# Packed attention and a gated feed-forward layer: halves of 288 tokens, a new order of steps, four stores from two engines

## The chip, the cores and the metric

The kernel runs on one core of a Trainium2 chip. The metric is the time of one execution on the device in microseconds (us); for the kernel before it is the median of three runs.

TensorE (PE) multiplies matrices and puts the results into PSUM banks; VectorE (DVE), ScalarE (ACT) and GpSimdE (POOL) work on elements; DMA transfers are issued by instructions on the queue of an engine, here mostly that of SyncE (SP).

## What is computed

```python
def sm_attn(qq, kk, vv):
    s = scale * np.matmul(qq, kk.transpose(0, 1, 3, 2))
    a = np.exp(s - np.max(s, axis=-1, keepdims=True))
    return np.matmul(a / (np.sum(a, axis=-1, keepdims=True) + 1e-09), vv)

p_packed = sm_attn(p, k, v)             # 32 pack queries per head
out = sm_attn(q, p_packed, p_packed)    # q: 8 batches, 8 heads, 576 tokens, 64 wide
x = out.transpose(0, 2, 1, 3).reshape(4608, 512)
h = x @ w_in                            # 512 x 2048
g = h * (1.0 / (1.0 + np.exp(-1.702 * h)))
return g @ w_out                        # 2048 x 512
```

Everything is float32. The weights reach the kernel as 64-bit words, which it converts.

## The kernel before

**Precision.** Each large product is made of three matmuls: an operand is split into an upper part, rounded to the matmul's type (`g_upper`, a cast, L175 on ScalarE and L177 on VectorE), and a lower part, the rest (`g_lower`, a subtraction, L848, on VectorE or GpSimdE), and upper x upper, upper x lower and lower x upper are added up in PSUM.

**Tiling.** A batch is 576 tokens. Its attention runs with all 8 heads at once: scores of the 32 pack queries (`scores1`, matmuls L369), their softmax, the packed values, then the scores of q against these (`scores2_mm`, L624, into the two banks of `hh`), transposed on VectorE (`scores2_turn`, L632) for the second softmax. `m_chunk` (L590) multiplies the packed values with `w_in`, so that h comes straight from the softmax weights. The q tokens of a batch are worked in two **halves**, `NH = (NA, NB_)` = 256 and 320 tokens.

Batch 0 runs while the weights are still loading, with steps of its own (`h_mm`, `h_tanh`, `h_gate`, `out_mm`). From batch 1 on, a **round** n = 2 to 15 is one half (batch n // 2, half n % 2), and in it a **pair** p = 0 to 7 is 256 of the 2048 columns of h. For each pair:

- `hp_mm` (twice): 6 matmuls (L705, in `h_terms`) into `hh`, of which there is one, with two banks;
- `hp_tanh` (ScalarE, L811) reads `hh` and writes the buffer of g in SBUF; `hp_gate` (VectorE, L698) multiplies it with `hh`, and after that `hh` is free;
- `hp_over` (a DMA on SP, L821) copies 64 tokens of the 320 to DRAM (`over_kept`), 56 times in all, in the odd rounds;
- `sums_1` to `sums_3` (L833, L837, L841), `g_upper`, `g_lower` prepare the operands; `product` (L870) multiplies 256 tokens by blocks with `w_out` into the four banks `acc`, in seven block products (15 pairs in four plain ones, `plain`);
- at the end of a round `take_1` to `take_6` (L894 to L918) add up `acc` in SBUF and `keep` (L924) stores 256 tokens.

The 64 left-over tokens of four batches are 256 again: rounds `('over', 0)` and `('over', 1)` read them back (`over_in`, L825) and end in `keep_over` (L929), four stores of 64 tokens each.

The buffers of g are a ring of two: pair i uses buffer i % 2, so `hp_tanh` of pair p + 2 waits until pair p's `hp_over` has been read out.

**What sets the order.** No scheduler: all steps stand in a table `order` of (step, arguments), written out in full, and are issued in that order. An engine takes its instructions in the order of the table, as does SP its DMAs: loads of q, k and v (`load`, L215 to L229) and of the weights (`load_w`, L259), their conversion (`begin_w`, ScalarE, L267; `join_w`, VectorE, L280), `w_kept` (a copy of `w_in` in DRAM, read back for every batch by `win_in`, L301), the transposed scores by way of DRAM (`aside`, L494 and L505) and all stores. `warm` (L181) is a matmul of the identity whose result nobody reads.

Of the kernel before, what the change touches and what calls it, by code (L numbers as in the profile page):

```python
# [19 lines left out]
P = 128  # L20
# [4 lines left out]
def kernel(  # L25
    ctx: ExitStack,
    tc: tile.TileContext,
    q0: bass.AP,
    q1: bass.AP,
# [10 lines left out]
    B = q0.shape[0]  # L40
# [5 lines left out]
    NH = (NA, NB_)  # L46
    S = NA + NB_
    REST = NB_ - NA
    NF = DF // P
# [29 lines left out]
    A = [region(4 * NA), region(4 * NB_)]  # L79
# [3 lines left out]
    X = [region(n) for n in (S, 2 * NB_, 2 * NB_, 2 * NB_, 2 * NB_)]  # L83
# [7 lines left out]
    DEC = region(3 * FC + 3 * NB_ + 64)  # L91
# [3 lines left out]
    SPARE = region(DM)  # L95

    G_RAW = 2 * NB_ + 4 * P
    G_PART = 7 * P + REST
# [64 lines left out]

    def rows(eo):
        return slice(eo * D, (eo + 1) * D)
# [24 lines left out]
    def kq_view(what, b):  # L190
# [7 lines left out]
        if what == "k":  # L198
            kq["p", b] = words(at, NP * NPK).rearrange("p (j n) -> p j n", n=NPK)
            at += NP * NPK  # L200
            n = (KF, S - KF)
        else:
            n = NH
# [5 lines left out]
    def load(what, b, part):  # L209
# [402 lines left out]
    def x2(b, half, eo=None):  # L612
        t = x_tile(X2.get((b, half), (0, 1)[half]), 2 * NH[half])
        return even_odd(t, eo)

    def xt(b, half, eo=None):
        t = x_tile(XT.get((b, half), (2, 4)[half]), 2 * NH[half])
        return even_odd(t, eo)

    def scores2_mm(b, half, banks):  # L620
        banks = [bank(i) for i in banks]
        for j in range(NP):
            for eo in range(2):
                nc.tensor.matmul(  # L624
                    banks[eo][32 * j : 32 * j + 32, : NH[half]], pt(b)[rows(eo), j, :],
# [4 lines left out]
    def scores2_turn(b, half, eo):  # L630
        t = st["bank", 2, b, half][eo]
        nc.vector.transpose(x2(b, half, eo), t[:, : NH[half]])  # L632
# [11 lines left out]
    def small2(name, b, half, eo):  # L644
        return even_odd(small((name, half), 2 * NH[half] // NPK), eo)
# [27 lines left out]
    def a_part(b, half, part, eo=None):  # L673
        at = A_FIRST if (b, half) == (0, 0) else A[half]
        n = 2 * NH[half]
# [5 lines left out]
    def a_lower_mm(b, half, eo, i):  # L681
        st["al", b, half, eo] = t = bank(i)
        n = NH[half]
# [3 lines left out]
    def a_lower_copy(b, half, eo, engine=nc.scalar):  # L687
        move(engine, a_part(b, half, 1, eo), st["al", b, half, eo][:, : NH[half]])
# [11 lines left out]
    def h_terms(t, b, f, half):  # L700
# [9 lines left out]
    def th0(f, half):  # L710
        return words(TH0 + TH_HOME[f][half] * NB_, NH[half])
# [8 lines left out]
    def h_tanh(b, f, half):  # L720
        nc.scalar.activation(th0(f, half), st["h", f, half][:, : NH[half]], AF.Tanh, scale=1.702)

    def h_gate(b, f, half):
        g = th0(f, half)
        gate(g, g, st["h", f, half][:, : NH[half]])

    def h_part(f, half):
        return th0(f, half)[:, NH[half] - NA :]
# [43 lines left out]
    def g_lead(n):  # L772
        return REST if isinstance(n, int) and n % 2 else 0
# [31 lines left out]
    def hp_view(n, p):  # L805
        k = NH[n % 2]
# [119 lines left out]
    def keep_over(n, i, k, engine=nc.sync):  # L926
# [7 lines left out]
        (warm, 1, 1, 5), (load, 'k', 0, 0), (warm, 7, 7, 4), (load, 'k', 0, 1), (load_w, 1, 0),  # L934
        (load_w, 0, 0), (load, 'v', 0, 0), (warm, 6, 2, 5), (load, 'v', 0, 1), (warm, 5, 2, 5),
        (load, 'q', 0, 0), (warm, 3, 3, 4), (load_w, 2, 0), (warm, 0, 3, 5), (load, 'q', 0, 1),
        (scores1, 0, 0, (6, 0)), (max1_first, 0, 0), (max1_first, 1, 0), (scores1, 0, 1, (7, 1)),
        (load_w, 3, 0), (bias1_first, 1), (bias1_first, 0), (exp1_first, 0, 0), (warm, 4, 2, 4),
        (load_w, 3, 1), (max1_first, 1, 1), (exp1_first, 1, 0), (warm, 8, 3, 4), (bias1, 0, 1),
        (load_w, 4), (max1_first, 0, 1), (exp1_first, 1, 1), (turn1_first, 0, 6), (bias1, 0, 0),  # L940
        (exp1_first, 0, 1), (begin_w, 1, 0), (turn1_first, 1, 7), (turn1_first_copy, 0, dve),
        (factor_first, 1), (begin_w, 0, 0), (sum1, 0, 1), (factor_first, 0), (turn1_last_mm, 0, 6),
        (turn1_first_copy, 1), (load, 'k', 1, 0), (pack_first, 0), (sum1, 0, 0),
# [976 lines left out]
```

## Time and profile before

| | us |
|---|---|
| median of three runs | 704.24 (704.01 to 705.41) |
| the profiled execution | 705.11 |
| its span in the trace | 703.3 |
| TensorE busy | 675.4 |
| VectorE busy | 567.5 |
| GpSimdE busy | 292.3 |
| ScalarE busy | 283.2 |

The trace is of one execution, and the span runs from the first recorded instruction to the last; 1.8 us lie around it. "Busy" is the time in which an engine has an instruction under way. The granted clock (PEclk) is given as a share of full speed; its mean over the span is 0.986. A wait is put down to the engine, tile and line that released it. A duration "x12" stands for twelve instructions in a row.

### The profile page before, as it was taken

Reading aid. Unit: us, or ns where it says so; the run is one execution under the profiler, and the core shown is the slowest. Engines: PE = TensorE matmul, PEld = TensorE weight load, DVE = VectorE, ACT = ScalarE, POOL = GpSimd, SP = SyncE. Lnnn points to the kernel's source line nnn. Section 1 sums busy time; section 2 is a strip of 40 time slices with the busy share of each in tenths; the row PEclk is TensorE's granted clock in tenths of the full one; section 3 lists DMA queues with packets and bytes.
Section 4 is the critical chain, followed back from the end, with each engine's and each line's share of the span. In section 5 each row is a group of like instructions: output and inputs, shape, how many; then the busy total and the mean of one; then the engine's idle time right before and its main releaser. Section 6 shows DMA issues by size and latency. Waiting matters only on the chain.

```text
span 703.3 us, 15452 instructions
## 1 busy us (share of the span) xinstructions
PE 675.4 (96%) x6037; PEld 602.3 (86%) x6037; DVE 567.5 (81%) x1123; ACT 283.2 (40%) x561; POOL 292.3 (42%) x325
## 2 busy tenths in 40 slices
PE   8799999999999999999999999999989999999996
PEld 6477767797879888899799998899879997899996
DVE  3999798885988898876998777977689778877785
ACT  3586644432453335324433334432335224333231
POOL 1434242322785446402534335553346325444232
PEclk9699999999999999999999999999999999999999
DMA  9869666324545425524451642534543632300142
GB/s 347 356 247 315 214 188 233 92 44 138 203 129 132 137 74 204 172 69 145 146 180 65 178 133 86 206 74 164 173 143 101 192 113 80 116 31 13 46 124 61
DMA packets 79017, 103.10 MB, mean 147 GB/s; under 512 B 53920, under 2 KB 58976, under 8 KB 74336
## 3 DMA queue, kind: packets, MB, share of 16 engines
q1 hardware_dynamic: 78944, 102.12, 45.0%
q8 instruction: 47, 0.77, 0.4%
q14 instruction: 26, 0.21, 0.1%
HBM read 80.14 MB, written 21.95 MB: 145 GB/s over the span
## 4 chain that ended last, share of the span: by engine, by line
PE 46%; DVE 10%; DMA 4%; issue 2%; ACT 2%; POOL 2%; DVEq 0%; SPq 0%; ACTq 0%; POOLq 0%
PE acc L870 28%; PE hh L705 15%; DMA over<-at_float 3%; DVE at_float L698 2%; DVE at_float32r L848 2%; PE b L590 2%; ACT at_float L811 1%; DVE at_float32r L177 1%; DMA at_float<-over 1%; PE hh L624 1%; DVE at_float L900 1%; PE hh L369 1%; DVE at_float32r L605 1%; ACT at_float32r L175 1%; POOL at_float L833 1%
## 5 line engine op out<-in xcount | busy, mean ns | idle before, releaser
L870 PE MATMUL acc<-at_float32r 128*128 128x256 f32 (+1 forms) x2553 | 361.2, 293 | 2.2 <-DVE at_float L918 1.1
L870 PEld LDWEIGHTS acc<-at_float32r 128*128 128x128 f32 x2553 | 330.8, 191 | 31.0 <-issue 14.6
L705 PE MATMUL hh<-at_float32r 128*128 128x256 f32 (+1 forms) x1344 | 208.4, 299 | 5.8 <-DVE at_float L632 2.7
L705 PEld LDWEIGHTS hh<-at_float32r 128*128 128x128 f32 x1344 | 186.9, 190 | 14.4 <-DVE at_float L698 5.4
L811 ACT ACTIVATE at_float<-hh 128x512 f32<-128x512 f32 (+1 forms) x112 | 72.9, 651 | 208.1 <-PE hh L705 132.2
L175 ACT CAST at_float32r<-at_float 128x512 fp32r<-128x512 f32 (+5 forms) x199 | 110.1, 567 | 99.9 <-PE acc L870 47.0
L848 POOL TENSOR_TENSOR at_float32r<-at_float,at_float32r 128x512 fp32r<-128x512 f32 (+3 forms) x82 | 102.3, 1251 | 91.3 <-DVE at_float32r L177 45.8
L698 DVE SCALAR_TENSOR_TENSOR at_float<-at_float,hh 128x512 f32<-128x512 f32 (+1 forms) x112 | 84.0, 750 | 56.9 <-ACT at_float L811 54.6
L848 DVE TENSOR_TENSOR at_float32r<-at_float,at_float32r 128x512 fp32r<-128x512 f32 (+3 forms) x159 | 109.4, 699 | 10.5 <-ACT at_float32r L175 7.1
L177 DVE CAST at_float32r<-at_float 128x512 fp32r<-128x512 f32 (+5 forms) x126 | 56.0, 449 | 8.6 <-PE acc L870 2.9
L837 POOL TENSOR_TENSOR at_float<-at_float 128x128 f32<-128x128 f32 x52 | 27.9, 537 | 82.5 <-DVE at_float L833 72.3
L833 POOL TENSOR_TENSOR at_float<-at_float 128x256 f32<-128x256 f32 x41 | 34.1, 831 | 62.6 <-DVE at_float L698 43.0
L755 PE MATMUL acc<-at_float32r 128*128 128x512 f32 x192 | 50.5, 399 | 0.7 <-DVE at_float32r L750 0.7
L841 POOL TENSOR_TENSOR at_float<-at_float 128x128 f32<-128x128 f32 x52 | 27.5, 529 | 46.4 <-DVE at_float L837 44.3
L755 PEld LDWEIGHTS acc<-at_float32r 128*128 128x128 f32 x192 | 34.0, 188 | 12.2 <-issue 3.4
L605 DVE TENSOR_TENSOR at_float32r<-b,at_float32r 128x512 fp32r<-128x512 f32 (+1 forms) x64 | 41.9, 669 | 1.4 <-ACT at_float32r L175 1.3
L833 DVE TENSOR_TENSOR at_float<-at_float 128x256 f32<-128x256 f32 x72 | 33.7, 468 | 4.6 <-DMA at_float<-over 1.5
L175 ACT CAST at_float32r<-b 128x512 fp32r<-128x512 f32 (+1 forms) x49 | 26.8, 574 | 24.9 <-PE b L590 24.8
L705 PEld LDWEIGHTS h<-at_float32r 128*128 128x128 f32 x192 | 30.0, 203 | 7.5 <-DVE at_float L698 2.3
L705 PE MATMUL h<-at_float32r 128*128 128x256 f32 (+1 forms) x192 | 32.8, 315 | 2.5 <-DVE at_float32r L605 1.1
L590 PE MATMUL b<-at_float,at_float 64*32 64x512 f32 (+1 forms) x512 | 34.6, 586 | 0.0
L280 DVE SCALAR_TENSOR_TENSOR at_float<-at_float,at_float 128x512 uint32<-128x512 uint32 (+1 forms) x36 | 29.7, 848 | 2.1 <-ACT at_float L267 2.0
(122 smaller groups left out, 556.8 us busy)
## 6 DMA issues: line engine op xcount, KB each, us to landing
at_float<-w_kept SPq DMA_DIRECT2D x24, 1024.0 KB, 5.1
at_float<-v SPq DMA_DIRECT2D x8, 1024.0 KB, 5.8
o<-at_float SPq DMA_DIRECT2D x32, 256.0 KB, 2.7
at_float<-w_out SPq DMA_DIRECT2D x16, 511.8 KB, 5.2
at_float<-w_in SPq DMA_DIRECT2D x12, 511.8 KB, 7.5
at_float<-k_last SPq DMA_DIRECT2D x8, 640.0 KB, 6.9
at_float<-q SPq DMA_DIRECT2D x8, 640.0 KB, 5.5
at_float<-pk SPq DMA_DIRECT2D x8, 576.0 KB, 4.3
```

Of the source, the lines that this page charges most:

```text
L175: nc.scalar.copy(dst, src)
L177: engine.tensor_copy(dst, src)
L280: nc.vector.scalar_tensor_tensor(dec(n)[:, at].bitcast(U32), raw(n)[:, at, 0], 13, tops[(n + (part or 0)) % 4][:, at], op0=ALU.logical_shi ...
L590: nc.tensor.matmul(banks[eo][32 * j : 32 * j + 32, columns(part)], pt(b)[rows(eo), j, :], w[rows(eo), j, columns(part)], start=True, stop= ...
L605: nc.vector.tensor_tensor(lo, t[:, at], hi.bitcast(F32), op=ALU.subtract)
L698: nc.vector.scalar_tensor_tensor(dst, th, 1.0, h, op0=ALU.add, op1=ALU.mult)
L705: nc.tensor.matmul(t[:, : NH[half]], m_part(fc, eo, mp)[:, fo : fo + P], a_part(b, half, ap, eo), start=(n == 0), stop=(n == len(terms) - 1),)
L755: nc.tensor.matmul(acc[i], g0(f, gp)[:, i * P : (i + 1) * P], wo(f, wp), start=(start and n == 0), stop=(stop and n == 2),)
L811: nc.scalar.activation(g, h, AF.Tanh, scale=1.702)
L833: engine.tensor_tensor(dst, src, by, op=ALU.subtract)
L848: engine.tensor_tensor(lo, src, g_range(n, p, 0, which)[0].bitcast(F32), op=ALU.subtract)
L870: nc.tensor.matmul(acc[i][:, at : at + m], lhs, rhs, start=(start and k == 0), stop=(stop and k == len(pairs) - 1),)
```

## The change

Four things are changed.

1. *Halves.* Batch 0 keeps 256 and 320 tokens; from batch 1 on both halves are 288. Each half now has 32 left-over tokens in place of 0 and 64, so `hp_over` runs for every pair of all rounds: 112 copies, each of 256 pieces of 128 bytes (before 56, with pieces of 256 bytes). q comes as one array, with the left-over tokens at the front of each half.
2. *Regions.* Some regions of SBUF get other sizes to suit.
3. *The order.* The first 230 steps come from a table of another version, not from the one shown here, and the others are in a new order; the two tables part from the first step on. TensorE issues 5171 instructions in both, VectorE 1125 and then 1141, ScalarE 545 and 571, GpSimdE 330 and 290, SP 332 and 386. `g_lower` runs 159 times on VectorE and 82 times on GpSimdE before, 175 and 66 times after.
4. *Last stores.* Of the four `keep_over` of the last round, two are issued by ScalarE.

```diff
+    HALF_REST = S // 2 - NA
...
-    A = [region(4 * NA), region(4 * NB_)]
+    A = [region(2 * S), region(4 * NB_)]
...
-    SPARE = region(DM)
-
-    G_RAW = 2 * NB_ + 4 * P
-    G_PART = 7 * P + REST
+    SPARE = region(S)
+
+    G_RAW = S + 4 * P
+    G_PART = 7 * P + HALF_REST
...
+    def halves(b):
+
+        return (S // 2, S // 2) if b else (NA, NB_)
...
-        elif part == 0:
-            nc.sync.dma_start(words(at, NP * NA), q0[b])
         else:
-            nc.sync.dma_start(words(at + NP * NA, NP * NB_), q1[b])
+            m = NP * halves(b)[0]
+            a, e = (m, NP * S) if part else (0, m)
+            nc.sync.dma_start(words(at + a, e - a), q[b][:, a:e])
...
-                t[:, : NH[half]], m_part(fc, eo, mp)[:, fo : fo + P], a_part(b, half, ap, eo),
+                t[:, : halves(b)[half]], m_part(fc, eo, mp)[:, fo : fo + P], a_part(b, half, ap, eo),
...
     def g_lead(n):
-        return REST if isinstance(n, int) and n % 2 else 0
+        return HALF_REST if isinstance(n, int) else 0
...
-        k = NH[n % 2]
+        k = halves(n // 2)[n % 2]
...
     def hp_over(n, p):
         b = n // 2
-        g = hp_view(n, p)[0][:, :, :REST]
+        g = hp_view(n, p)[0][:, :, :HALF_REST]
+        r = slice(n % 2 * HALF_REST, (n % 2 + 1) * HALF_REST)
         dst = over_kept[b // 4][p].rearrange("p (j t) b r -> p j t b r", t=2)
-        nc.sync.dma_start(dst[:, :, b % 4 // 2, b % 2, :], g)
+        nc.sync.dma_start(dst[:, :, b % 4 // 2, b % 2, r], g)
...
-        (keep_over, ('over', 1), 1, 1), (keep_over, ('over', 1), 0, 1),
+        (keep_over, ('over', 1), 1, 1, act), (keep_over, ('over', 1), 0, 1, act),
```

Behind the change the same steps have line numbers that are higher by 3 to 5 (`warm` L184, `scores1` L372, `h_terms` L709, `hp_over` L826, `keep_over` L934). In the rows of the order below, `h`, `b` and `acc` are PSUM banks, and `at_float` with a number is a region of SBUF.

**TensorE at the start.** Before, 18 warm-up matmuls stand ahead of the first scores (the matmuls that read the region of k):

```order
L181 MATMUL h_73<-at_float_74 128x128
L181 MATMUL h_72<-at_float_74 128x128 x7
L181 MATMUL h_73<-at_float_74 128x128 x4
L181 MATMUL h_72<-at_float_74 128x128 x3
L181 MATMUL h_73<-at_float_74 128x128 x3
L369 MATMUL b_67<-at_float_98 32x256
L369 MATMUL acc_63<-at_float_98 32x256
```

After:

```order
L184 MATMUL h_72<-at_float_74 128x128 x7
L372 MATMUL b_67<-at_float_104 32x256
L372 MATMUL acc_63<-at_float_104 32x256
L372 MATMUL b_67<-at_float_104 32x256
L372 MATMUL acc_63<-at_float_104 32x256
```

Eleven warm-ups have gone from there.

**TensorE ahead of the first product with the weights** (L593, `m_chunk`), after; the row ahead of the warm-ups is the last of the scores of q. Before, only three warm-ups stood at this place:

```order
L627 MATMUL acc_66<-at_float_113,at_float_232 32x320
L184 MATMUL h_73<-at_float_74 128x128 x2
L184 MATMUL h_72<-at_float_74 128x128 x3
L184 MATMUL h_73<-at_float_74 128x128 x3
L184 MATMUL h_72<-at_float_74 128x128 x3
L593 MATMUL acc_63<-at_float_243,at_float_232 32x256
L593 MATMUL acc_64<-at_float_243,at_float_232 32x256
```

The warm-ups stand now between the scores of q and the product with the weights.

**SP at the start**, the loads in the order in which they are issued, before (pk is the pack queries with the first 256 keys):

```order
L221 DMA at_float_98<-pk 128x1152
L223 DMA at_float_98<-k_last 128x1280
L259 DMA at_float_108<-w_in 128x1023
L259 DMA at_float_110<-w_in 128x1023
L215 DMA at_float_112<-v 128x2048
L217 DMA at_float_113<-v_last 128x512
L227 DMA at_float_120<-q 128x1024
L259 DMA at_float_125<-w_in 128x1023
L229 DMA at_float_120<-q 128x1280
```

After:

```order
L224 DMA at_float_104<-pk 128x1152
L226 DMA at_float_104<-k_last 128x1280
L218 DMA at_float_107<-v 128x2048
L262 DMA at_float_110<-w_in 128x1023
L220 DMA at_float_108<-v_last 128x512
L232 DMA at_float_113<-q 128x1024
L232 DMA at_float_113<-q 128x1280
L262 DMA at_float_116<-w_in 128x1023
L262 DMA at_float_126<-w_in 128x1023
```

Values and q have moved ahead of two pieces of `w_in`.

**SP in round 11**, before: the copies to `over` of its pairs 0 to 3 between the loads of the next q and two stores of output:

```order
L821 DMA over_95<-at_float_350 256x1x64
L229 DMA at_float_98<-q 128x1280
L821 DMA over_95<-at_float_350 256x1x64
L924 DMA o<-at_float_1226 128x512 x2
L227 DMA at_float_98<-q 128x1024
L821 DMA over_95<-at_float_350 256x1x64 x2
```

After (the first row is its pairs 0 and 1, the `aside` rows are the reads of the transposed scores):

```order
L826 DMA over_95<-at_float_350 256x1x32 x2
L508 DMA at_float_92<-aside_5077 32x4x256
L508 DMA at_float_92<-aside_5077 32x256
L508 DMA at_float_92<-aside_5077 32x4x256 x3
L508 DMA at_float_92<-aside_5077 32x256
L826 DMA over_95<-at_float_350 256x1x32
L232 DMA at_float_104<-q 128x1152 x2
L826 DMA over_95<-at_float_350 256x1x32 x2
```

Three copies stand now ahead of the loads of q, and the stores of output have left this place.

## Rows read from the trace of the kernel before

**Rows 1.** The page: busy time, share and instructions of each engine.

```profile
PE 675.4 (96%) x6037; PEld 602.3 (86%) x6037; DVE 567.5 (81%) x1123; ACT 283.2 (40%) x561; POOL 292.3 (42%) x325
```

**Rows 2.** Windows: us, busy PE, PEld, DVE, ACT, POOL, PEclk, DMA share, GB/s.

```profile
0.00:28.40 28.40, 20.84 (x246) 15.06 (x246) 16.70 (x48) 13.38 (x38) 7.80 (x18) 0.87 0.95 373
28.40:697.70 669.30, 654.55 (x5791) 587.21 (x5791) 550.15 (x1075) 269.79 (x523) 284.45 (x307) 0.99 0.43 137
```

**Rows 3.** What TensorE waited for: us in total, times, longest us.

```profile
PE hh L624 <- DVE at_float L698: 5.0, 6, 1.5
PE hh L705 <- DVE at_float L632: 2.7, 3, 1.9
```

**Rows 4.** `hp_over`, L821: ns min/median/max of an issue; who waited (us, times).

```profile
L821 SPq DMA_DIRECT2D over<-at_float x56: 512/525/972, 151.6 to 669.6; - x56
...
  ACT at_float L811: 14.7, 4
```

**Rows 5.** Timeline of TensorE: start us, us, line, tile, [idle before, releaser].

```profile
170.79 0.45 PE L624 MATMUL hh<-at_float,at_float 64*32 64x256 f32 x8 [0.85 <-DVE at_float L698]
...
517.94 0.85 PE L705 MATMUL hh<-at_float32r 128*128 128x320 f32 x4 [1.93 <-DVE at_float L632]
```

**Rows 6.** Timeline of TensorE from 398 to 410 us.

```profile
400.60 1.60 PE L705 MATMUL hh<-at_float32r 128*128 128x256 f32 x12
402.04 1.96 PE L870 MATMUL acc<-at_float32r 128*128 128x256 f32 x15
...
405.07 1.04 PE L705 MATMUL hh<-at_float32r 128*128 128x320 f32 x6
405.96 2.31 PE L870 MATMUL acc<-at_float32r 128*128 128x256 f32 x18
```

**Rows 7.** The page: DMA issues, KB each, median us from issue to landing.

```profile
over<-at_float SPq DMA_DIRECT2D x64, 64.0 KB, 2.7
aside<-at_float SPq DMA_DIRECT2D x56, 72.0 KB, 2.5
```

**Rows 8.** Timeline of TensorE from 0 to 40 us.

```profile
1.37 7.05 PE L181 MATMUL h<-at_float 128*128 128x128 f32 x36 [1.37 <-POOL at_float masks.py:199]
8.35 0.40 PE L369 MATMUL b<-at_float 64*32 64x256 f32 x1
...
16.46 0.75 PE L624 MATMUL acc<-at_float,at_float 64*32 64x320 f32 x16
...
21.16 0.64 PE L590 MATMUL acc<-at_float,at_float 64*32 64x256 f32 x2 [2.31 <-DVE at_float L280]
```

**Rows 9.** Timeline of SP: the first two issues.

```profile
0.75 0.40 SPq L221 DMA_DIRECT2D at_float<-pk  x1
1.20 0.42 SPq L223 DMA_DIRECT2D at_float<-k_last  x1
```

**Rows 10.** DMA issues from 0 to 6 us: KB each, us from issue to landing.

```profile
at_float<-k_last SPq DMA_DIRECT2D x1, 640.0 KB, 5.0
at_float<-q SPq DMA_DIRECT2D x1, 640.0 KB, 10.1
at_float<-pk SPq DMA_DIRECT2D x1, 576.0 KB, 3.9
```

**Rows 11.** Windows, columns as in rows 2.

```profile
32.00:34.00 2.00, 2.00 (x10) 2.00 (x9) 1.75 (x3) 1.29 (x3) 1.48 (x2) 0.50 0.34 137
520.00:522.00 2.00, 2.00 (x11) 2.00 (x11) 0.61 (x1) 1.18 (x2) 0.00 (x0) 0.50 1.00 412
```

**Rows 12.** Groups by line and shape: count, busy us, mean ns, idle before.

```profile
L848 DVE TENSOR_TENSOR at_float32r<-at_float,at_float32r 128x512 fp32r<-128x512 f32 x76 | 55.6, 732 | 6.2 <-ACT at_float32r L175 3.6 <-DVE at_float32r L177 0.5
L848 POOL TENSOR_TENSOR at_float32r<-at_float,at_float32r 128x512 fp32r<-128x512 f32 x46 | 61.0, 1325 | 49.7 <-ACT at_float32r L175 24.3 <-DVE at_float32r L177 21.6 <-DMA at_float<-over 2.5
```

**Rows 13.** Timeline of SP at the end: the four stores of `keep_over`.

```profile
698.13 2.43 SPq L929 DMA_DIRECT2D o<-at_float  x4
```

**Rows 14.** Windows of 20 us, columns as in rows 2.

```profile
40.00:60.00 20.00, 20.00 (x120) 16.31 (x119) 19.53 (x42) 17.39 (x39) 8.20 (x8) 1.00 0.95 336
```

More of the change, by code (lines that the diff above doesn't have):

```diff
@@ L202, in kq_view @@
         else:
-            n = NH
+            n = halves(b)
         kq[what, b] = [
@@ L644, in small2 @@
     def small2(name, b, half, eo):
-        return even_odd(small((name, half), 2 * NH[half] // NPK), eo)
+        t = small((name, half), 20 if half else 18)
+        return even_odd(t[:, : 2 * halves(b)[half] // NPK], eo)
     def max2(b, half, eo=None):
@@ L687, in a_lower_copy @@
     def a_lower_copy(b, half, eo, engine=nc.scalar):
-        move(engine, a_part(b, half, 1, eo), st["al", b, half, eo][:, : NH[half]])
+        move(engine, a_part(b, half, 1, eo), st["al", b, half, eo][:, : halves(b)[half]])
     def a_lower(b, half, engine=nc.gpsimd):
@@ new lines @@
+        (conv_upper, 0, -1, dve),
+        (both, (scores2_mm, 3, 0, (4, 5)), (m_chunk, 3, 0, (6, 7), None)), (conv_lower, 0, 1, dve),
+        (hp_over, 5, 3), (g_lower, 5, 2, 1, dve), (keep, 4, 0), (sums_1, 5, 4, dve),
+        (g_upper, 5, 3, 0, dve), (m_upper, 3, 0, 0, None, act), (win_in, 3, 1), (product, 5, 1, 6),
+        (scores2_turn, 3, 0, 0), (g_lower, 5, 3, 0, pool), (product, 5, 2, 6),
+        (scores2_turn, 3, 0, 1), (hp_mm, 5, 5, 0), (m_upper, 3, 0, 1, None, dve),
+        (conv_lower, 0, -1, pool), (hp_mm, 5, 5, 1), (sums_2, 5, 3, dve), (max2, 3, 0),
@@ new lines @@
+        (sums_3, 9, 1, dve), (take_5, 8), (pack, 5, (6, 7)), (g_upper, 9, 1, 1, act),
+        (g_upper, 9, 0, 1, act), (keep, 8, 1), (hp_tanh, 9, 3), (g_lower, 9, 0, 1, dve),
+        (load, 'q', 5, 0), (product, 9, 0, 2), (product, 9, 1, 1), (pack_end, 5), (hp_gate, 9, 3),
+        (sums_1, 9, 2, pool), (product, 9, 0, 4), (product, 9, 0, 6), (hp_over, 9, 3),
+        (sums_2, 9, 2, dve), (hp_mm, 9, 4, 0), (g_lower, 9, 1, 1, dve), (product, 9, 1, 2),
+        (g_upper, 9, 2, 0, dve), (hp_mm, 9, 4, 1), (g_lower, 9, 2, 0, dve), (sums_3, 9, 2, dve),
@@ new lines @@
+        (both, (scores2_mm, 5, 1, (4, 5)), (m_chunk, 5, 1, (6, 7), None)), (g_upper, 9, 4, 1, act),
+        (g_lower, 9, 5, 0, pool), (turn2, 5, 0), (a_upper, 5, 0, None, act),
+        (g_lower, 9, 4, 1, dve), (sums_3, 9, 5, pool), (scores2_turn, 5, 1, 1),
+        (m_upper, 5, 1, 1, None, act), (load, 'k', 6, 1), (product, 9, 3, 7), (product, 9, 4, 1),
+        (scores2_turn, 5, 1, 0), (keep, 8, 0), (hp_mm, 9, 7, 1), (sums_1, 9, 6, dve),
+        (hp_over, 9, 6), (a_lower, 5, 0, dve), (win_in, 5, 2), (product, 9, 4, 4),
@@ new lines @@
+        (hp_over, 12, 0), (product, 11, 5, 4), (sum2, 6, 1), (hp_over, 11, 7),
+        (both, (scores1, 7, 0, (4, 5)), (m_chunk, 6, 2, (6, 7), None)), (load, 'k', 7, 1),
+        (scores1_copy, 7, 0, 0, act), (m_upper, 6, 2, 0, None, dve), (win_in, 6, 3),
+        (product, 11, 6, 4), (g_upper, 11, 7, 0, act), (product, 11, 5, 6), (keep, 10, 0),
+        (g_upper, 12, 0, 0, dve), (scores1_copy, 7, 0, 1, act), (hp_mm, 12, 1, 0),
+        (g_lower, 11, 7, 0, dve), (m_upper, 6, 2, 1, None, act), (g_lower, 12, 0, 0, pool),
```

1892 lines of the change are left out of this document (945 added, 947 removed).

## The prediction

> **What bounds the kernel now.** I read the page first: TensorE is counted busy for 675.4 of 703.3 us, VectorE for 567.5, and no other engine for half the span [rows 1]. Then the sums by stretch: up to 28.4 us TensorE is busy for 20.84 us and the DMA engines for 0.95 of the time; from there to the last matmul, at 697.7 us, it idles for 669.30 - 654.55 = 14.75 us; the last 5.6 us (703.3 - 697.7) are the final sums and stores [rows 2]. So the three stages have different limits: a chain of loads and small operations at the start, TensorE with a few pauses in the middle, stores at the end. The middle can give back 14.75 us at most, unless a matmul becomes cheaper.
>
> The table of waits tells what ends those pauses: nearly always VectorE, with the gate (L698), which frees the `hh` bank, ahead of all (5.0 us ahead of L624 alone), then the transposes of the scores (L632, 2.7 us) [rows 3]. Behind several gates stands a DMA. The tanh writes into a ring of buffers from which `hp_over` is still being copied to DRAM, and ScalarE waited for those copies four times, 14.7 us in all [rows 4]. I found the copies in the trace's DMA issues: they belong to rounds 3, 7, 11 and 13, and each was issued right behind loads of q, a weight load or stores of output. Behind those four waits TensorE stood for 0.85, 1.04, 0.49 and 1.51 us, 3.9 us together (the first in [rows 5]).
>
> **The change, part by part.** *Halves of 288.* The 1344 matmuls of `hp_mm` go from 256 or 320 columns to 288. Twelve of 256 start 1.44 us before what follows (400.60 to 402.04), 0.120 us each; six of 320 take 0.89 us (405.07 to 405.96), 0.148 us each [rows 6]. Two of 288 between those ends take 0.268 us for 0.268: zero. If the step at 288 lay at either end it would be 1344 x 0.014 = 19 us less or more; I take the straight line. Tanh, gate, casts and sums keep their mean length in the same way, since the columns of two halves add up to the same 576.
>
> *Twice as many `hp_over`.* 56 stores of 64-float pieces become 112 of 32-float pieces; each also costs one issue on SyncE. SyncE is not short of time: a store is issued in a median of 0.525 us [rows 4], and 54 more instructions are some 28 us of 700. What counts is when they land. A store of 256-byte pieces lands in a median of 2.7 us, one of 128-byte pieces (`aside`) in 2.5 us, although it has 576 of them to 256 [rows 7]. So a single store gets no slower. In the order of before, round 11 has a q load ahead of the second `hp_over` and two output stores and a second q load ahead of the third; in the new order three `hp_over` go out before the first q load, and the tanh that waits for the fourth is some 8 us of matmuls away. With both tables laid side by side, I count TensorE's steps from each store to the tanh that reuses its buffer, and take off 2 us and the transfer time of what is queued right ahead: 15 of 56 had under 1 us to spare, now 10 of 111. At the old rate the waits would double, +3.9 us; without any it is -3.9 us. I take -2.9, one wait left of four.
>
> *The start.* Before, 36 records of warm-up matmuls hold TensorE from 1.37 to 8.4 us, and the first scores start at 8.35 [rows 8], though the first keys, issued at 0.75, had landed 3.9 us later, at 4.65, and the second, issued at 1.20, after 5.0, at 6.2 [rows 9, 10]. In the new order 7 warm-ups stand ahead instead of 18, so both pairs of scores go as the keys land: 3.7 and 2.6 us earlier. What is late next: the values and q, which move ahead of two quarter-megabyte pieces of weight (0.7 us each at the rate of the stretch, 373 GB/s [rows 2]); the second q, which took 10.1 us from issue to landing [rows 10] and was there before the scores against it, at 16.46 [rows 8], comes those 1.4 us earlier. Then the first product with the weights: it waited 2.31 us, up to 21.16, for a join on VectorE [rows 8], not for a load, and the last of its four pieces keeps its place in the queue. I take 3.0 us for the whole chain up to where TensorE stays busy (28.4 before [rows 2]). The bounds: TensorE ran at half its clock (0.50, 1.2 GHz) from about 21 to 34.5 us (a stretch of it in [rows 11]). The warm-ups that leave the head go into the pause ahead of the weight product. If they hold the clock up, half of the 6 us of dense half-speed work comes back too: -6. If the thin stretch ahead of them stays at half speed, the bursts of scores, transposes and packing take some 2.5 us longer: -0.5.
>
> *The rest of the order.* TensorE has 5171 instructions in both; ScalarE gets 26 more, VectorE 16 more, GpSimdE 40 fewer. Sixteen of the subtractions `g_lower` go from GpSimdE (1.325 us) to VectorE (0.732) [rows 12]. Those alone are 11.7 us more for VectorE and 21 us less for GpSimdE; with the smaller moves I estimate 17 more and 46 less. VectorE has 669.30 - 550.15 = 119 us idle in the middle [rows 2], which covers it on average. I take +1, with 0 to +12 as bounds. Once, before 517.94, TensorE stood 1.93 us behind transposes [rows 5], and the clock then fell to half (0.50 in 520 to 522 [rows 11]; with the stretches beside it some 1.7 us lost): 3.6 together. The new order may meet its like elsewhere: 0 to -3.6, I take -1.
>
> *Last four stores.* SyncE issues them in 2.43 us from 698.13 [rows 13], 0.6 us each. From two engines the last issue starts 1.2 us earlier. If the transfers and not the issues space the landings, little is left: -0.3 to -1.2, I take -0.9.
>
> **Sum.** The profiled execution took 705.11 us (span 703.3, 1.8 around it), 0.87 above the median 704.24. -3.0 - 2.9 + 1.0 - 1.0 - 0.9 = -6.8, so 698.3 beside the profiled one and 697.4 beside the median: 697.5.
>
> **Rivals.** *The start is given back.* From 40 to 60 us VectorE is busy for 19.53 of 20 us [rows 14]: batch 0 could hang on it, and TensorE be early for nothing. For it: that row. Against: VectorE's own chain starts 3 us earlier too. Price: the 3.0, so 700.5.
>
> *The waits for `hp_over` double.* Every round now has them, also those that load k and v. For it: 4 of 56 waited. Against: the count of spare time above. Price: +3.9 in place of -2.9, 704.3, no change. The Trainium skill (DMA: Bandwidth & Descriptors, "Why small descriptors are slow (HBM only)") speaks for it: a fixed cost per piece makes a 256-byte piece 11 cycles, and by the same sum 7 for 128 bytes, so twice the pieces would cost 27% more DMA time for the same data. No row shows that cost apart; by the rule alone the sum would stand with this rival, by the landings in [rows 7] with the forecast.
>
> *VectorE falls behind (slower).* The 16 subtractions that it gets stand where it is already full, as it is in [rows 14], and TensorE waits for each gate queued behind one: 16 x 0.732 = 11.7 us in place of the 1.0, 708. It decides from where VectorE's idle time in a 20 us stretch falls under about 1 us. Against: only one more stretch of 20 us in the whole span shows over 19, and GpSimdE's load falls.
>
> *288 does not lie on the line,* so that a half costs what 320 does: +19 us, 716.5. Nothing in [rows 6] points to it.
>
> **Chances.** Forecast 0.62, start given back 0.15, waits doubled 0.08, VectorE behind 0.12, 288 off the line 0.03. The forecast's own range is 691 to 702, from the bounds of the start (-6 to -0.5), the waits, the clock and VectorE. Taking in the second and third case gives 690 to 704.5 and leaves out 0.15 above and some 0.03 below. A measurement tells 0.2%, 1.4 us, from no change. Faster than that: 0.62 + 0.15 = 0.77; within it 0.08; slower 0.12 + 0.03 = 0.15.
>
> **What would show it.** Right: the first scores near 4.7 us, TensorE dense from about 25; the wait of the tanh for `over` under 5 us in total; TensorE idle in the middle under 12 us; the last stores issued in pairs from two engines, under 4.5 us from the last sum to the end. Wrong: steps of 288 off 0.134 us; VectorE above 19 of 20 us in several stretches with pauses of TensorE behind L698 or its `g_lower`; a tanh that waits for `over` in the even rounds; the clock at half for most of the first 40 us.

## The result and the profile after

The changed kernel takes 680.39 us (median of four runs, 678.84 to 685.86); the kernel before, beside it, 704.12. The ratio is 0.9675 (95% interval 0.9619 to 0.9730). A second set of runs, with another five runs of the changed kernel, gave 0.9671 (0.9647 to 0.9695). So it is 22 to 24 us faster, more than three times what was forecast, and below the stated range. The profiled execution took 680.52 us, its span is 678.7.

First the page's busy times, then the same two stretches as in [rows 2] (the second one up to the last matmul):

```profile
PE 662.1 (98%) x6037; PEld 593.2 (87%) x6037; DVE 558.1 (82%) x1139; ACT 295.7 (44%) x585; POOL 242.5 (36%) x285
```

```profile
0.00:28.40 28.40, 24.25 (x285) 16.14 (x285) 19.09 (x57) 16.66 (x45) 9.58 (x19) 1.00 0.95 368
28.40:672.97 644.57, 637.76 (x5754) 577.05 (x5752) 538.11 (x1082) 279.05 (x541) 232.90 (x266) 1.00 0.46 143
```

TensorE idles in the middle for 644.57 - 637.76 = 6.81 us, against 14.75 [rows 2]. With the first stretch, idle time fell from (28.40 - 20.84) + 14.75 = 22.3 us to (28.40 - 24.25) + 6.81 = 11.0. That is 11 us of 24; the other 13 lie inside "busy". The granted clock is 1.00 in both stretches; it was 0.87 and 0.99. VectorE's busy time *falls* by 9.4 us, though it has 16 instructions more, and GpSimdE's by 49.8.

The two falls belong together. In before, a `g_lower` of 128x512 on VectorE took 687 ns in the 53 cases in which GpSimdE ran no tensor operation beside it, and 834 ns on average in the 23 others. The gate of 128x512, which reads `hh` in PSUM, took 683 and 680. The joins of the weights show it most. Before, 14 of 28 ran beside GpSimdE and took 1113 ns on average, the others 681; now 11 do and take 777, the others 686. The first row is before, the second after:

```profile
L280 DVE SCALAR_TENSOR_TENSOR at_float<-at_float,at_float 128x512 uint32<-128x512 uint32 x28 | 24.6, 897 | 2.1 <-ACT at_float L267 2.0
L283 DVE SCALAR_TENSOR_TENSOR at_float<-at_float,at_float 128x512 uint32<-128x512 uint32 x28 | 19.9, 722 | 5.2 <-ACT at_float L270 5.2
```

If each of VectorE's instructions is held against the median of its like without GpSimdE beside it, the lengthening adds up to 51 us in before, 28 in the change and 43 in `a_split` (below), an estimate from the starts and lengths in the traces.

What TensorE waited for (us, times, longest), to be held against [rows 3], and who waited for a copy `hp_over` (L826 now; [rows 4]):

```profile
PE hh L709 <- DVE at_float L635: 1.1, 3, 0.4
PE hh L627 <- DVE at_float32r L180: 0.9, 1, 0.9
PE hh L627 <- DVE at_float L702: 0.8, 2, 0.7
```

```profile
L826 SPq DMA_DIRECT2D over<-at_float x112: 512/525/1949, 102.8 to 643.9; - x112
...
  ACT at_float L815: 6.9, 3
```

The gates (L702) held TensorE up for 0.8 us ahead of the scores of q, before for 5.0; the transposes (L635) for 1.1, before 2.7. ScalarE waited 6.9 us for copies instead of 14.7, and behind that stands one pause of TensorE, of 0.68 us.

To see where the time went I took a second measure, since short waits are not counted as idle. Each matmul has a usual distance to the next (66 ns for 128 columns, 120 for 256, 133.6 for 288, 147.3 for 320, 231 for 512, for the small ones what they cost in their groups). The sum of these is the work, 640.4 us in every kernel here; the **lag** is the start of a matmul less the work ahead of it. Worked out from the starts of all matmuls in the traces (four of the columns are experiments of the next section: `x_halves`, `b_start`, `x_order2` and `a_split`):

| work done, us | before | halves alone | start alone | order alone | the change | the change, old split |
|---|---|---|---|---|---|---|
| 16 | 22.4 | 22.0 | 15.5 | 14.9 | 15.3 | 15.1 |
| 32 | 23.3 | 23.0 | 23.1 | 17.0 | 16.3 | 16.3 |
| 120 | 28.8 | 28.2 | 27.5 | 19.1 | 18.2 | 18.4 |
| 280 | 38.8 | 38.1 | 37.5 | 24.9 | 21.8 | 25.6 |
| 440 | 45.1 | 45.8 | 44.6 | 31.0 | 27.5 | 35.5 |
| 480 | 50.5 | 51.0 | 48.6 | 32.0 | 28.6 | 37.8 |
| 639 | 57.0 | 57.7 | 56.9 | 39.5 | 32.5 | 46.2 |

The change is 7.1 us ahead when the start is over, 10.6 at 120, 17 at 280, and gains another 4 between 440 and 480, where the kernel before had its pause before 517.94 [rows 5] and half a clock behind it [rows 11]. It is not one place: the lag grows more slowly nearly everywhere.

### The profile page after: what moved, and what is told of

Same layout as the page of the kernel before. It is cut to its first block, busy times and chain, and to the rows that moved or that the text cites. A ratio compares the mean times of both kernels' runs of the same rounds, so it can differ in the third digit from the quotient of the medians.

```text
span 678.7 us, 15627 instructions
## 1 busy us (share of the span) xinstructions
PE 662.1 (98%) x6037; PEld 593.2 (87%) x6037; DVE 558.1 (82%) x1139; ACT 295.7 (44%) x585; POOL 242.5 (36%) x285
## 3 DMA queue, kind: packets, MB, share of 16 engines
q1 hardware_dynamic: 94016, 101.86, 47.5%
## 5 line engine op out<-in xcount | busy, mean ns | idle before, releaser
L875 PEld LDWEIGHTS acc<-at_float32r 128*128 128x128 f32 x2553 | 326.6, 188 | 29.1 <-issue 17.4
L709 PE MATMUL hh<-at_float32r 128*128 128x288 f32 x1344 | 206.5, 297 | 2.0 <-DVE at_float L635 1.1
L709 PEld LDWEIGHTS hh<-at_float32r 128*128 128x128 f32 x1344 | 185.4, 188 | 8.4 <-DVE at_float L635 1.9
L178 ACT CAST at_float32r<-at_float 128x512 fp32r<-128x512 f32 (+6 forms) x217 | 120.0, 570 | 100.7 <-PE acc L875 58.1
L815 ACT ACTIVATE at_float<-hh 128x576 f32<-128x576 f32 x112 | 73.1, 653 | 181.1 <-PE hh L709 119.9
L853 DVE TENSOR_TENSOR at_float32r<-at_float,at_float32r 128x512 fp32r<-128x512 f32 (+3 forms) x175 | 116.9, 676 | 18.8 <-ACT at_float32r L178 15.7
L702 DVE SCALAR_TENSOR_TENSOR at_float<-at_float,hh 128x576 f32<-128x576 f32 x112 | 84.2, 752 | 43.5 <-ACT at_float L815 38.6
L853 POOL TENSOR_TENSOR at_float32r<-at_float,at_float32r 128x512 fp32r<-128x512 f32 (+3 forms) x66 | 82.4, 1253 | 100.4 <-DVE at_float32r L180 52.2
L180 DVE CAST at_float32r<-at_float 128x416 fp32r<-128x416 f32 (+6 forms) x108 | 47.0, 437 | 8.0 <-POOL at_float L846 3.8
L759 PEld LDWEIGHTS acc<-at_float32r 128*128 128x128 f32 x192 | 34.5, 188 | 9.8 <-issue 2.5
L838 DVE TENSOR_TENSOR at_float<-at_float 128x256 f32<-128x256 f32 x80 | 38.6, 485 | 4.9 <-POOL at_float32r L853 1.9
L838 POOL TENSOR_TENSOR at_float<-at_float 128x256 f32<-128x256 f32 x33 | 26.7, 810 | 37.1 <-DVE at_float32r L853 22.0
L846 POOL TENSOR_TENSOR at_float<-at_float 128x128 f32<-128x128 f32 x44 | 24.0, 547 | 40.0 <-DVE at_float L842 38.8
L593 PE MATMUL b<-at_float,at_float 64*32 64x512 f32 (+1 forms) x512 | 34.0, 586 | 0.7 <-DMA at_float<-w_kept 0.7
L709 PEld LDWEIGHTS h<-at_float32r 128*128 128x128 f32 x192 | 27.5, 189 | 5.9 <-DVE at_float L702 1.2
L709 PE MATMUL h<-at_float32r 128*128 128x256 f32 (+1 forms) x192 | 30.3, 300 | 1.0 <-DVE at_float32r L608 0.4
L754 POOL TENSOR_TENSOR at_float32r<-at_float,at_float32r 128x256 fp32r<-128x256 f32 x19 | 16.1, 852 | 38.1 <-ACT at_float32r L178 27.3
```

The lines of the kernel that those rows point to most:

```text
L178: nc.scalar.copy(dst, src)
L180: engine.tensor_copy(dst, src)
L593: nc.tensor.matmul(banks[eo][32 * j : 32 * j + 32, columns(part)], pt(b)[rows(eo), j, :], w[rows(eo), j, columns(part)], start=True, stop= ...
L702: nc.vector.scalar_tensor_tensor(dst, th, 1.0, h, op0=ALU.add, op1=ALU.mult)
L709: nc.tensor.matmul(t[:, : halves(b)[half]], m_part(fc, eo, mp)[:, fo : fo + P], a_part(b, half, ap, eo), start=(n == 0), stop=(n == len(te ...
L759: nc.tensor.matmul(acc[i], g0(f, gp)[:, i * P : (i + 1) * P], wo(f, wp), start=(start and n == 0), stop=(stop and n == 2),)
```

## The experiments

Ratios are to the kernel before on the same chip in the same set of runs.

**The parts alone.** `x_halves` has the code of the change and the order of before, with the missing copies put in:

```diff
         (hp_gate, 2, 0), ...
+        (hp_over, 2, 0),
```

(56 times.) The 64 left-over tokens of batch 0 are not computed as in the reference; all other work is.

> The changed kernel's code with halves of 288 tokens, but the order of the kernel before; the 56 copies hp_over that the even rounds now need stand four steps behind their gate, which is the median distance in both tables, and the last four stores are on SyncE. Theory 'order' (the new table makes TensorE wait less, the halves are neutral): 702 to 707 us, no change against before. Theory 'halves' (two equal halves per batch pace the gates better and their steps of 133 ns are cheaper than 120 and 147): about 687 us, which is the measured gain of 24 less the 7 that the traces put into the first 28 us. In the trace, both expect steps of 128x288 at 133 ns.

Measured: 705.47 us, 0.9994 (0.9972 to 1.0017). No change, as theory "order" had it, but not because nothing happens. The products get faster, though their 256 columns are the same. These are the products' rows in before, `x_halves` and the change (by line and shape: count, busy us, mean ns of one):

```profile
L870 PE MATMUL acc<-at_float32r 128*128 128x256 f32 x2373 | 315.8, 285 | 1.1 <-DVE at_float32r L848 0.8
```

```profile
L875 PE MATMUL acc<-at_float32r 128*128 128x256 f32 x2373 | 313.6, 283 | 3.5 <-DVE at_float32r L853 2.3 <-DVE at_float L918 0.9
```

```profile
L875 PE MATMUL acc<-at_float32r 128*128 128x256 f32 x2373 | 311.7, 283 | 0.9 <-DVE at_float32r L853 0.7 <-DVE at_float L918 0.2
```

From start to start (steps without a wait) a product takes 119.65 ns with halves of 256 and 320 and 118.4 with halves of 288, in either order; `hp_mm` takes 132.1 to 132.4 in place of a mean of 133.1. Over 2373 and 1344 matmuls that is some 4 us. In `x_halves` waits take this back: ScalarE now waited six times for copies,

```profile
  ACT at_float L815: 15.9, 6
```

and TensorE's idle time in the middle is 17.6 us (669.80 - 652.19), against 14.75.

`x_order` is the reverse: the code of before and the new order without the 56 copies of the even rounds.

```diff
-        (hp_over, 2, 0),
```

In it and in `x_order2` the first 64 to 128 tokens of batches 3 to 7 are not computed as in the reference.

> The kernel before with halves of 256 and 320 tokens, but in the new order (the copies hp_over of the even rounds left out, as these rounds have none; the last stores from two engines). Theory 'order': 680 to 684 us, the whole gain. Theory 'halves': about 697 us, the gain of the start alone. If the order is tuned to halves of 288 and loses on 256 and 320 because a gate comes late in every second round, 685 to 695 us with waits of TensorE behind L698 of over 5 us.

Measured: 694.53 us, 0.9851 (0.9806 to 0.9895), as the third line of the expectation has it, but for another reason than a late gate: TensorE stood 3.45 us behind `w_kept` at 327.7.

```profile
327.72 1.96 PE L590 MATMUL b<-at_float,at_float 64*32 64x512 f32 x16 [3.45 <-DMA at_float<-w_kept]
```

With these halves q's second part overlays the next pack queries, and the new order loads those first. `x_order2` moves three loads:

```diff
-        (load, 'k', 5, 0),
         (both, (scores2_mm, 4, 1, (4, 5)), (m_chunk, 4, 1, (6, 7), None)),
+        (load, 'k', 5, 0),
```

> The new order with halves of 256 and 320 once more, with three loads of keys (batches 3, 5 and 6) moved behind the second scores of q, since with these halves they overlay q and made the loads wait in x_order, where TensorE stood 3.45 us behind w_kept at 327.7 us. A small part of the output (the first 64 to 128 tokens of batches 3 to 7) is not computed as the reference has it; the instructions are the same. Theory 'order alone gives most' (the pause at 327.7 was made by the overlay): 684 to 689 us. Theory 'order and halves only work together': 692 to 695 us as in x_order, with pauses elsewhere.

Measured: 687.16 us, 0.9755 (0.9732 to 0.9778): the order alone gives 17 us, at the middle of "order alone gives most". The halves, worth nothing in the old order, are worth another 6 in the new one (0.9755 to 0.9671). The 4 us of shorter steps and a few pauses would make up that much, which is argued, not shown.

**The start.** `b_warm` moves only the 26 warm-ups of before to the places of the new table; `a_warm` moves those of the change back.

```diff
-        (warm, 1, 1, 5), (load, 'k', 0, 0), (warm, 7, 7, 4), (load, 'k', 0, 1), (load_w, 1, 0),
+        (warm, 7, 7, 4), (load, 'k', 0, 0), (load, 'k', 0, 1), (load_w, 1, 0),
...
+        (warm, 5, 2, 5), (warm, 8, 3, 4), (warm, 0, 3, 5), (warm, 2, 3, 4),
         (m_chunk, 0, 0, (0, 1), 0),
```

> The kernel before, with its 26 warm-up matmuls moved to where the new table has them: 7 ahead of the first scores instead of 18, 11 ahead of the first product with the weights instead of 3, the others between. Nothing else is moved, the loads neither. Theory 'warm-ups' (scores start as the keys land, and warm-ups in the later pause keep the granted clock at 1.0, so that nothing runs at 0.5 from 21 to 34.5 us): 697 to 699 us. Theory 'rest of the first 230 steps' (loads and ScalarE/VectorE order set the start): 702 to 704 us with the clock at 0.5 in 24 to 34 us as before.

> The changed kernel with its 26 warm-ups moved back to where the kernel before has them (18 ahead of the first scores, 5 ahead of the first transposes, 3 ahead of the first product with the weights). Theory 'warm-ups': 685 to 688 us, and the clock falls to 0.5 again near 20 us. Theory 'rest of the first 230 steps': 680 to 682 us.

Measured: `b_warm` 702.71 us, 0.9970 (0.9946 to 0.9994); `a_warm` 683.46, 0.9701 (0.9654 to 0.9748). At the end of the start the lag differs by 3 us from its kernel in both traces. By the times `b_warm` gains 2 us, between its two theories; for `a_warm` they don't tell, as its interval takes in the change's 0.9671. The windows from 25 to 30 us (columns as in rows 2), of before, `b_warm`, `a_warm` and the change:

```profile
25.00:30.00 5.00, 3.31 (x18) 2.19 (x24) 4.75 (x10) 3.08 (x9) 1.26 (x1) 0.50 1.03 421
```

```profile
25.00:30.00 5.00, 4.31 (x28) 3.07 (x29) 4.52 (x8) 1.87 (x7) 1.87 (x2) 0.50 1.03 418
```

```profile
25.00:30.00 5.00, 5.00 (x35) 3.81 (x35) 4.60 (x11) 3.49 (x9) 3.12 (x3) 0.63 1.02 416
```

```profile
25.00:30.00 5.00, 4.91 (x51) 3.03 (x50) 4.82 (x13) 3.94 (x10) 2.27 (x3) 1.00 1.03 417
```

Only with the new warm-ups and the new rest together does the granted clock stay at 1.00. In before it was at the lower of the two levels (1.2 GHz, 0.50) from 20.9 to 34.5 us. In `b_warm` it still fell, at 23.8 us, with TensorE busy for 2.27 us from 20 to 25, and came back at 30.6; in `a_warm` it was down from 21.9 to 28.7.

`b_start` puts the first 230 steps of the new table, with their engines, in front of the rest of the old order.

```diff
-    order = ( ...the old table... )
+    order = ( ...230 steps of the new table, then the old table without them... )
```

> The kernel before with only its beginning changed: the first 230 steps of the new table, with their engines, in front, and all other steps behind them in the old order. Theory 'the start is 7 us, by itself' (the lag of the two traces at 40 us): 697.5 us, and PEclk 1.0 from 20 to 35 us. Theory 'part of it needs the later order' (VectorE, full from 40 to 60 us, takes some back): 699 to 702 us.

Measured: 705.05 us, 1.0008 (0.9988 to 1.0027): no gain, which neither theory had. The start is as early as in the change (lag 15.5 at 16 us of work, clock 1.00 up to 40 us), and then everything is lost at one place, right behind the seam. TensorE's and ScalarE's timeline there:

```profile
42.67 1.04 PE L705 MATMUL h<-at_float32r 128*128 128x320 f32 x6
48.85 1.43 PE L705 MATMUL h<-at_float32r 128*128 128x256 f32 x5 [5.14 <-DVE at_float L698]
```

```profile
44.03 0.76 ACT L267 CAST at_float<-at_float 128x512 f16<-128x512 bf16 x1 [0.53 <-DMA at_float<-w_out]
46.92 0.76 ACT L267 CAST at_float<-at_float 128x512 f16<-128x512 bf16 x1 [2.13 <-DMA at_float<-w_out]
48.16 0.77 ACT L267 CAST at_float<-at_float 128x512 f16<-128x512 bf16 x1 [0.48 <-DMA at_float<-w_out]
```

Conversions of `w_out` pieces (`begin_w`, L267) stand ahead on ScalarE, and VectorE's `join_w` ahead of a gate; they wait for pieces that land at 44.0, 46.9 and 48.1 us, with the DMA engines full since the start. TensorE waits behind them for 5.14 us, and the clock is at 0.50 from 46.1 to 52.9 us. In `x_order2` the pieces land at nearly the same times (44.1, 46.1, 47.8), but there other work stands in front, and TensorE waits 1.4 us. So here the early start was worth something only with an order behind it that has work for TensorE while the next weights land.

**The pauses of before, repaired.** `b_five` changes the old order at five places:

```diff
-        (load, 'q', 6, 1),
         (hp_over, 11, 1),
+        (load, 'q', 6, 1),
```

(and in the same way `hp_over` (3, 2), (7, 4) and (13, 2), with the stores and loads ahead of them; `scores2_turn` of (6, 1) goes ahead of `sums_2`, `g_upper` and `turn2` on VectorE.)

> The kernel before, with nothing but SyncE's and VectorE's order changed at five places: at the four where ScalarE waited for a copy hp_over, the loads and stores that stood right ahead of it go behind it; and the transposes scores2_turn of the second half of batch 6 go ahead of the sums and casts that kept TensorE waiting until 517.94 us. Theory 'each pause is worth what the trace shows': 0.85 + 1.04 + 0.49 + 1.51 + 1.93 us and 1.7 us of half clock behind the last, 7.5 us in all: 697 us against 704.5, and PEclk 1.0 at 520 us. Theory 'given back' (the next gate or load is late next): 701 to 704 us, with pauses of the same size a few us further on.

Measured: 700.78 us, 0.9946 (0.9929 to 0.9963): 3.8 us of 7.5, between its two theories. ScalarE's waits for copies fell from 14.7 us to 1.0, and the clock stayed up: from 519 to 521 us, before and `b_five`,

```profile
519.00:521.00 2.00, 2.00 (x11) 2.00 (x10) 0.93 (x2) 0.35 (x1) 0.00 (x0) 0.55 1.02 381
```

```profile
519.00:521.00 2.00, 1.84 (x15) 1.84 (x16) 2.00 (x5) 0.63 (x2) 0.74 (x1) 1.00 1.06 408
```

But the first place got worse, as the load of q that had gone behind the copy now came late itself (1.30 us instead of 0.85 [rows 5]), and of the 1.04 us at 339 it kept 0.45:

```profile
170.99 0.67 PE L624 MATMUL hh<-at_float,at_float 64*32 64x256 f32 x16 [1.30 <-DMA at_float<-q]
```

**The engines.** `a_split` keeps the sequence of the change and gives 88 subtractions back to the engine that did them before:

```diff
-        (g_lower, 3, 0, 0, dve),
+        (g_lower, 3, 0, 0, pool),
```

> The changed kernel, in which each of the 88 subtractions g_lower that the two tables give to different engines (52 that went from GpSimdE to VectorE, 36 the other way) is back on the engine of the kernel before; the sequence stays. Theory 'split' (the gain of some 10 us in the middle is in the choice of engines): 688 to 692 us. Theory 'sequence': 682 to 684 us, and TensorE's waits behind VectorE's gate stay under 4 us.

Measured: 692.50 us, 0.9823 (0.9794 to 0.9852): some 10.5 us slower than the change, with nothing changed but the choice of engines. One chain shows in ScalarE's waits, `a_split` first, then the change: the tanh waits until a subtraction on GpSimdE has read the buffer of g that it is to overwrite.

```profile
ACT at_float L815 <- POOL at_float32r L853: 17.9, 10, 4.0
```

```profile
ACT at_float L815 <- POOL at_float32r L853: 3.5, 2, 2.1
```

The longest of these waits in `a_split`, from the subtraction by way of the tanh and the gate to TensorE:

```profile
410.19 1.34 POOL L853 TENSOR_TENSOR at_float32r<-at_float,at_float32r 128x416 fp32r<-128x416 f32 x1 [1.36 <-DVE at_float32r L180]
411.56 0.65 ACT L815 ACTIVATE at_float<-hh 128x576 f32<-128x576 f32 x1 [3.95 <-POOL at_float32r L853]
412.24 0.75 DVE L702 SCALAR_TENSOR_TENSOR at_float<-at_float,hh 128x576 f32<-128x576 f32 x1 [1.22 <-ACT at_float L815]
413.05 0.72 PE L627 MATMUL hh<-at_float,at_float 64*32 64x288 f32 x16 [0.94 <-DVE at_float L702]
```

This chain is not the whole of it. Both kernels issue the same matmuls in the same order; held against each other one by one, `a_split` loses, after the start and counting single places of over 0.35 us, 5.9 us in front of matmuls into `hh` (behind gates, transposes, a cast and a load of q), and 5.5 in front of products, which wait for a rounded operand or for a bank of `acc`. VectorE's operations beside GpSimdE also take 15 us more in sum (28 and 43 us above). How the 10.5 us divide among the late buffer, the slower subtraction and the lengthened work of VectorE is not shown. Nor is it shown whether the new engines would help the old sequence: no run has that.

A subtraction of 128x512 takes 1.33 us on GpSimdE and 0.71 on VectorE there. The Trainium skill (Trainium Architecture — The Big Picture, "The five engines, in one table") calls GpSimdE two times slower than VectorE in streaming elementwise work; the rows give 1.9 for this shape.

**Addresses.** `b_part` is before with the parts of the rounded g 992 words apart, `a_part` and `a_part2` the change with 960 and 992:

```diff
-    G_PART = 7 * P + REST
+    G_PART = 7 * P + REST + 32
```

> The kernel before with G_PART, the distance of the parts of the rounded g buffers in SBUF, of 992 words instead of 960: nothing else changes but addresses. In the traces a product matmul of 256 columns starts every 119.65 us-thousandths (ns) with halves of 256 and 320, and every 118.4 ns with halves of 288, whatever the order. Theory 'placement' (the addresses of the g blocks, which the sizes of the halves set, make the difference): 118.4 ns, 701 us. Theory 'the mix of lengths': 119.65 ns as before, 704.5 us.

> The changed kernel with G_PART, the distance of the parts of the rounded g buffers, of 960 words in place of 928; only addresses change. Theory 'placement by G_PART' (960 is the kernel before's value, and 992 there took the product's step from 119.65 to 118.95 ns): the step goes up to about 119.6 ns, 3 us slower than after2. Theory 'alignment of the blocks inside a part' (lead of 32 instead of 0 and 64 words): the step stays at 118.4 ns, no change.

> The same with G_PART of 992 words. Theory 'placement by G_PART': 118.4 to 119 ns, within 1.5 us of after2. Theory 'alignment of the blocks inside a part': 118.4 ns, no change.

> The changed kernel once more, as the measure for the runs beside it: 679 to 682 us, ratio 0.967, the granted clock 1.0 over the first 35 us and a product matmul of 256 columns every 118.4 ns, as in its first trace.

Measured: `b_part` 703.28 us, 0.9988 (0.9973 to 1.0004), with a product's step of 118.95 ns: in before the distance of the parts alone does a little over half of it; in time that is within the uncertainty. `a_part` 682.23 (0.9664), step 118.66; `a_part2` 681.59 (0.9651), 118.42; `after2`, the measure beside them, 682.90 (0.9671), 118.42, 0.9 us above what was expected of it. So the distance of the parts matters in before and hardly in the change; the offset of the blocks inside a part, which the halves set, must carry the rest. That is argued from what is left, not shown.

**Copies and tail.** `a_over2` issues each copy `hp_over` twice, `a_tail` puts the last four stores back on SyncE (the second piece of the diff).

```diff
+        dst = over_spare[b // 4][p].rearrange("p (j t) b r -> p j t b r", t=2)
+        nc.sync.dma_start(dst[:, :, b % 4 // 2, b % 2, r], g)
...
-        (keep_over, ('over', 1), 1, 1, act), (keep_over, ('over', 1), 0, 1, act),
+        (keep_over, ('over', 1), 1, 1), (keep_over, ('over', 1), 0, 1),
```

> The changed kernel with each of its 112 copies hp_over issued twice, the second time to a part of DRAM that nobody reads. The forecast's theory (in the new order the copies have room, and each costs SyncE 0.525 us and nothing on TensorE's path): within 1.5 us of after2. Rival 'waits double' (what lands behind them lands later, and ScalarE waits): 4 us and more slower, with waits of ScalarE for over of over 14 us.

> The changed kernel with all four last stores on SyncE again. The forecast's theory (issues space the landings): 0.9 us slower, 681.3 us. Rival (from the end of the last sum to the end of the span it is 4.86 us in the changed kernel and 4.92 before, so nothing was gained): no change, 680.4 us.

Measured: `a_over2` 687.38 us, 0.9734 (0.9704 to 0.9764), 4.5 us slower than `after2`: the rival's price, though by another way, for ScalarE waited only 3.8 us for the added copies. What grew are single pauses from 500 us on (1.9, 0.9 and 0.8 us); what causes each stays open. `a_tail` 681.29, 0.9683 (0.9658 to 0.9709): inconclusive. From the end of the last sum to the end of the span it is 4.92 us in before, 4.86 in the change, 5.36 in `a_tail`:

```profile
673.42 0.42 DVE L923 TENSOR_TENSOR at_float<-acc,at_float 128x256 f32<-128x256 f32 x1
673.60 1.20 ACTq L934 DMA_DIRECT2D o<-at_float  x2
673.87 1.20 SPq L934 DMA_DIRECT2D o<-at_float  x2
```

The issues do go out in half the time (1.2 us in place of 2.43 [rows 13]), but the end comes hardly sooner.

**A version beyond.** `a_best` takes `a_part2` and, in round 7, puts `w_kept` ahead of two transfers.

```diff
-        (load, 'k', 5, 0),
-        (keep, 6, 0),
         (win_in, 4, 1),
+        (load, 'k', 5, 0),
+        (keep, 6, 0),
```

> The changed kernel with G_PART of 992 words (a_part2) and, in round 7, the load of w_kept ahead of the next keys and of one store of output, as TensorE waited 0.7 to 1.0 us for it at 322.5. If each is worth what it seems: 1 to 2 us less than the changed kernel, ratio to before about 0.964; otherwise 0.967, no change.

Measured: 680.61 us, 0.9667 (0.9630 to 0.9704): no different from the change.

## Why the prediction was wrong

The direction was right and so were several of the mechanisms; most terms were too small, and one had the wrong sign. Against the sum, with the differences of the two traces (lag at the end: 57.0 - 32.5 = 24.5 us):

- *The start*, -3.0 taken, -7.1 measured, beyond the bound of -6. The scores did go as the keys landed (first matmuls of L372 at 4.65 us), and the weight product waited 0.43 us in place of 2.31 [rows 8]. The step that failed: I priced the half clock by "the 6 us of dense half-speed work" and kept it for the bound. In before TensorE was busy for 11.08 us at half clock (20.9 to 34.5 us), and in the change the clock never fell there. What the prediction missed altogether is that the 7.1 us hang on the order behind: alone they are given back (`b_start`), which is the first rival, with the weights' transfers and not VectorE as what is late next.
- *The waits for `hp_over`*, -2.9 taken. ScalarE's waits fell by 7.8 us, TensorE's behind them from 3.9 to 0.7: -3.2. That is right in size, but not in its signs: ScalarE's waits were to be under 5 us with one wait left, and were 6.9 us at three; the longest of them, 3.49 us, is in the even round 14, a sign that the forecast had named against itself. In `b_five` the repairs gave back 3.8 of the 7.5 us that the pauses promised, and `x_halves` shows that the rival was near: in the old order the doubled copies made six waits.
- *The rest of the order*, +1 for VectorE taken, with 0 to +12 as bounds: the wrong sign, and the largest error. What the other terms leave of the lag is 24.5 - 7.1 - 3.2 - 3.6 - 4.2 = 6.4 us gained, put down to pauses and short waits behind VectorE. The step that failed is "Those alone are 11.7 us more for VectorE", with the cost that was set on it. VectorE did not become busier: 558.1 us, before 567.5. Its instructions alone grew by 15 us by the estimate above, near the 17 that I had put, but the lengthening beside GpSimdE fell by 23. I priced the subtraction by the time that it takes from its engine, and not by what it does to the others: on VectorE it is done 0.6 us sooner for whoever waits, and less of VectorE's work runs long beside GpSimdE. `a_split` prices the choice of engines at 10.5 us in this sequence.
- *The clock and the transposes in the middle*, -1 taken of 0 to -3.6; all of it came: the pause before 517.94 is gone, and the granted clock is 1.00 from the start to the last matmul. That no pause of the kind came elsewhere was not foreseen by any count.
- *Halves of 288*, zero taken, -4.2 measured, for a reason that I had put at nothing: the products of 256 columns got 1.2 ns faster each, which no row of before could show, and the step at 288 is 132.1 ns, a little below the line. `b_part` shows that addresses can make a product faster; I had left the resized regions out of the sum. Whether the step at 288 is lower by its length or by its place is not shown.
- *The last stores*, -0.9 taken, -0.06 between the two traces, inconclusive in `a_tail`. From the last sum to the end it is 4.86 us, not under 4.5.

The rule of the Trainium skill on small pieces that the prediction weighed (DMA: Bandwidth & Descriptors, "Why small descriptors are slow (HBM only)") does not show in one copy's landing: the median from issue's end was 2.1 us with 256 bytes and 1.9 with 128. It shows in the page's queue row, which gives the DMA engines' time: 45.0% of 703.3 us before, 47.5% of 678.7 now, 5.9 us more on average of the 16, for 14,336 more pieces. The new order alone does not do that: `x_order2`, with 256 bytes, has 46.2% of 685.6 us, what before has. The 112 further copies of `a_over2` added 23.2 us (51.0% of 683.2 less 47.8% of 680.3 in `after2`), so, as an estimate from these rows, the same bytes took 17.3 us in pieces of 256 bytes and 23.2 in pieces of 128. That is a third more, beside the 27% that the prediction estimated from the rule. So pieces do cost; in the changed order TensorE stood for 0.68 us behind the copies.

The rivals: VectorE did not fall behind; 288 left the line on the good side. The range failed not only by single terms: even with all of them at their best bounds the forecast comes to 704.1 - 6 - 3.9 - 3.6 - 1.2 = 689.4 us, 9 above the measured time. The rest of the order was bounded at no gain, the halves were put at zero, and 14.75 us of idle time was taken for all that the middle could give; it gave 24.5 - 7.1 = 17.4. More than half of the measured gain came from inside "busy": matmuls at half clock, matmuls that a wait delayed by less than their overlap with the one before, and shorter steps.

## What to carry to other kernels

An engine with idle time looks like a place for work, but here a subtraction was worth what its *readers* and the *next owner of its buffer* gained, and what it did to the engine beside it, not what it took. So where a ring of buffers waits for a slow engine, try the faster one, even if that is the busier; and before counting its load, look in the trace whether its operations get longer when the other works beside it. Parts of a reordering didn't add up: the earlier start was worth nothing where the next weights were the next thing late, and equal halves paid only in an order that had room for their copies. Bound such a change by all the time in which TensorE runs below its own best step and at half clock, not by its idle gaps.

## What the hardware showed

- A matmul of 128x256 took 119.65 ns from start to start in one layout of SBUF and 118.4 in another, with the same operands' shapes, and 118.95 when only the distance of the parts of the rounded g went from 960 to 992 words (`b_part`).
- A subtraction of 128x512 on VectorE with its operands in SBUF took 687 ns with no tensor operation of GpSimdE beside it, and 834 ns on average with one (before, L848); a gate of 128x512 that reads PSUM took 683 and 680.
- The granted clock fell to 0.50 at 23.8 us in `b_warm`, where TensorE was busy for 2.27 us from 20 to 25, and at 46.1 us in `b_start`, inside a pause of 5.14 us. In the change it stayed at 1.00 until the last matmul.
- 112 additional copies of 32 KB in pieces of 128 bytes (`a_over2`), for which ScalarE waited 3.8 us, cost 4.5 us together.
